# Decode attention with a gated MLP on one core: the first column group of the output moves from partitions 0–3 to partitions 28–31

## The chip, the cores and the metric

The kernel runs on one core of a Trainium2 chip. The metric is device time in microseconds (us) of one execution, the median of several runs. Before the change it is 110.05 us, the median of 3 runs that lie between 110.0 and 110.17 us. One further execution was taken by the hardware profiler; all durations below are from it.

## What is computed

Two batch rows of 448 numbers go through a layer norm, a query projection, attention of 16 query heads over 8 key/value heads with a window of the last 2048 positions, and an output projection. A small MLP on the same normed rows gives a gate, and the output is the input plus attention times gate:

```
xn  = layernorm(x)                                  # x: 2 x 1 x 448
q   = xn @ wq                                       # 16 heads of 256
p   = softmax(q k^T / 16)  over the last 2048 keys  # 8 kv heads, each for 2 query heads
s   = (p v) @ wo                                    # 4096 -> 448
g   = silu( relu(xn @ w1) @ w2 )                    # 448 -> 1792 -> 448
out = x + s * g                                     # bfloat16
```

## The kernel before, in words

The kernel is written as five lists of instructions, one for each engine: TensorE (PE), VectorE (DVE), ScalarE (ACT), GpSimd (POOL) and SyncE (SP). Each instruction names the earlier ones that it depends on, and a small planner (`_Prog`) turns that into semaphores: a transfer has a semaphore of its own that counts to 16, a compute instruction adds one to its engine's semaphore. The order inside a list is the order in which it is written. All matrix products are recorded at one line (311) and all transfer issues at line 39.

**The loads** are all issued by SP in one queue, in this order: wq, w1, w2, four key tiles of 4 MB (two batch rows times two groups of four kv heads), the value tiles into the same buffers as soon as the scores of a tile are done (the last one in two halves), and at the end wo in five parts of 20, 4, 4, 3 and 1 blocks (`WO_PARTS`). ACT issues only the small loads: `x_sb`, the two input rows as they are, and `x_c`, the same rows in the layout of the output.

**The middle** does not change. DVE transposes the keys in place (line 346), PE makes the scores of four tiles, DVE and ACT do the softmax, PE multiplies with the values, and DVE scales the result.

**The layout of the output** is what the change touches. The 448 columns are cut into four groups of 112 (`NCOL`). Group c is written as c = 2k + h. The result lies in PSUM as two blocks of four partitions, one for each h, at partitions 32h to 32h+3; inside a block the partition is 2b + k, where b is the batch row. So partitions 0–3 hold the groups with h = 0, and partitions 32–35 those with h = 1, because a matrix product can write to a column strip of PE that begins at a multiple of 32. The vector work at the end runs over partitions 0 to 35 (`ROWS` = 36).

A row gets into its partition through the stationary operand. `at2` (line 231) holds for each of 32 blocks of wo five columns (`PADW`): 0, b=0, 0, b=1, 0. A slice of four columns that starts at 1 − k puts the two batch rows at places k and 2 + k, with zeros between them (line 540). `fpad` (line 215) is the same for a selection matrix in float32, which folds four partial sums that lie in four strips into one (lines 467 and 535). GpSimd clears both tiles at the start (line 268), as the last of six clears on which other instructions wait as `p_z`.

**The end of the kernel** (lines 520 to 552): the first 24 blocks of wo go through PE as four strips with both batch rows (line 525) into `wbk`; DVE copies that to `wc` (line 528). Then PE adds blocks 24 to 27 in the output's layout (line 540), folds `wc` in (line 535), and adds blocks 28 to 31. Each part of wo is waited for through `landed`. DVE multiplies with the gate (line 546), adds the input (line 548), and the result is stored by two transfers that are issued at the same time, one by SP and one by ACT (line 550), each with four rows of 224 bytes. SP waits for both (line 551), and that is the end of the program.

```
d_o = [pr.dma(eng, half(out, h), out_sb[32 * h:32 * h + 4, :], [v_o]) for h, eng in ((0, SP), (1, ACTE))]
pr.op(SP, None, d_o)
```

Of the kernel before, what the change touches and what calls it, by code (L numbers as in the profile page):

```python
# [5 lines left out]
BF = mybir.dt.bfloat16  # L6
F32 = mybir.dt.float32
# [4 lines left out]
PE, DVE, ACTE, SP, POOL = "pe", "dve", "act", "sp", "pool"  # L12
# [121 lines left out]
def bass_recurrent_scan__sliding_block_cached__dense_activation_relu__decode_kernel(  # L134
# [11 lines left out]
    B, Sq, D = A_x.shape  # L146
# [13 lines left out]
    FC = DFF // 2  # L160
    NCOL = D // 4
    ROWS = 36
    PADW = 5
    WO_PARTS = [20, 4, 4, 3, 1]
    WO_TILED = 24
    WO_FOLD = 28
# [2 lines left out]
    with es:  # L169
        pr = _Prog(nc, es)  # L170

        def named(name, shape, dt):
            return es.enter_context(nc.sbuf_tensor(name, shape, dt))

        def psum(name, shape, dt):
            return es.enter_context(nc.psum_tensor(name, shape, dt))

        def view(t, off, dims, n=128, p0=0):
            width = t.shape[1]
            return bass.AP(t, p0 * width + off, [[width, n]] + dims)  # L180
# [6 lines left out]
        wqo = named("wqo", [128, 32 * D], BF)  # L187
# [10 lines left out]
        f8 = named("f8", [128, 8], F32)  # L198
        asel = named("asel", [128, 72], BF)
        x_sb = named("x_sb", [128, D], BF)  # L200
        x_c = named("x_c", [128, NCOL], BF)
# [10 lines left out]
        h_sb = named("h_sb", [128, 448], BF)  # L212
        zc = named("zc", [128, D], F32)
        wc = named("wc", [128, D], F32)
        fpad = named("fpad", [128, PADW], F32)
        ea = named("ea", [128, NCOL], F32)
        g_sb = named("g_sb", [128, NCOL], F32)
        tmp = named("tmp", [128, NCOL], F32)
        out_sb = named("out_sb", [128, NCOL], BF)
# [8 lines left out]
        rs = named("rs", [128, 2 * NU], F32)  # L228
        pt = [named(f"pt{i}", [128, 512], BF) for i in range(NU)]
        o_odd = named("o_odd", [128, DH], F32)  # L230
        at2 = named("at2", [128, 32 * PADW], BF)

        sbk = [psum(f"sbk{i}", [128, 512], F32) for i in range(2)]
        obk = psum("obk", [128, 512], F32)
# [1 line left out]
        mbk = psum("mbk", [128, 512], F32)  # L236
        qbk = psum("qbk", [128, 512], F32)
        wbk = psum("wbk", [128, 512], F32)
        fbk = psum("fbk", [128, 512], F32)

        def half(t, h):
            return t.rearrange("b s (k h n) -> h (b s k) n", h=2, n=NCOL)[h]

        def kv_src(u, cache):
            b, hg = divmod(u, 2)
# [1 line left out]

        d_x = pr.dma(ACTE, x_sb[0:B, :], A_x[:, 0, :])
        p_xc = pr.op(POOL, lambda e: e.memset(x_c[:, :], 0.0))
        d_xc = [pr.dma(ACTE, x_c[32 * h:32 * h + 4, :], half(A_x, h), [p_xc]) for h in range(2)]  # L250
        wq_src = A_wq.rearrange("r (hf c) -> (r hf) c", hf=2).rearrange("(p s) c -> p (s c)", s=SLOTS)
        w1_src = B_w1.rearrange("r (hf c) -> (r hf) c", hf=2).rearrange("(p s) c -> p (s c)", s=SLOTS)
        w2_src = B_w2.rearrange("(p j) n -> p (j n)", j=14)
# [7 lines left out]
        for u in range(NU):  # L261
# [4 lines left out]
            out=ident[:, :], in_=ident[:, :], compare_op=ALU.not_equal, fill=1.0,  # L266
            base=0, pattern=[[-1, 128]], channel_multiplier=1), [i0])
        p_z = [pr.op(POOL, lambda e, t=t: e.memset(t[:, :], 0.0))
               for t in (fpad, asel, rm, bt, qstat, at2)][-1]
# [4 lines left out]
            out=sd[0:B, 0:1], in0=st2[0:B, 1:2], scalar1=EPS, scalar2=None, op0=ALU.add), [v_ag])  # L274
# [5 lines left out]
        def z(t):  # L280
            return a_z[t.name]

        def red(out, in_, axis=AX.X):
            def fn(e):
                with nc.allow_low_precision("zeros and ones"):
                    return e.tensor_reduce(out=out, in_=in_, axis=axis, op=ALU.add)
            return fn
# [4 lines left out]
        v_pm = pr.op(DVE, red(pmask[:, :], view(ident, 0, [[1, 4], [4, 32]])))  # L292
        v_g8 = pr.op(DVE, red(view(g8, 0, [[2, 4], [1, 2]]), view(ident, 0, [[32, 4], [1, 2], [2, 4]])))
        v_f8 = pr.op(DVE, red(f8[:, :], view(ident, 0, [[1, 8], [8, 16]])))
        v_fp = pr.op(DVE, lambda e: e.tensor_copy(view(fpad, 1, [[2, B]]), f8[:, 0:B]), [v_f8, p_z])
        v_h2 = pr.op(DVE, red(half2[:, :], view(ident, 0, [[8, 2], [16, 8], [1, 8]]), AX.XY))
        v_gs = pr.op(DVE, lambda e: e.tensor_copy(
            view(gsum, 0, [[8, 16], [1, 8]]), view(g8, 0, [[0, 16], [1, 8]])), [v_g8])
# [4 lines left out]
        for e2 in range(2):  # L303
            v_xn = pr.op(DVE, lambda e, e2=e2: e.tensor_scalar(
                out=view(xg, 128 - 127 * e2, [[256, 4], [128, 2], [2, 64]], n=B),
# [4 lines left out]
        def mm(out_ap, lhsT, rhs, start, stop=False, **kw):  # L310
            return lambda e: e.matmul(out_ap, lhsT=lhsT, rhs=rhs, start=start, stop=stop,  # L311
                                      skip_group_check=True, **kw)

        for s in range(SLOTS):
# [3 lines left out]
            out=view(xr, 0, [[4, SLOTS], [2, 2], [1, 2]]), in0=view(mbk, 0, [[2, SLOTS], [0, 2], [1, 2]]),  # L318
# [3 lines left out]
        deps = [d_wq, v_xr, z(qbk)]  # L322
        for s in range(SLOTS):
            for i in range(4):
                lo = s * HC + i * 512
                m_q = pr.op(PE, mm(qbk[32 * i:32 * i + 4, :], xr[:, 4 * s:4 * s + 4], wqo[:, lo:lo + 512],
                                   s == 0, s == SLOTS - 1, tile_position=(0, 32 * i)), deps)
                deps = []
        v_q = pr.op(DVE, lambda e: e.tensor_scalar(  # L329
            out=view(q_x, 0, [[256, 8], [128, 2], [1, 32]]), in0=view(qbk, 0, [[64, 8], [1, 2], [2, 32]]),  # L330
# [3 lines left out]
        deps = [v_qx, st["mbk"]]  # L334
        for n in range(16):
            m_qt = pr.op(PE, mm(mbk[:, 16 * n:16 * n + 16], q_x[:, 128 * n:128 * n + 128],
                                view(ident, 0, [[32, 4], [1, 4]]), n == 0), deps)
            deps = []
# [92 lines left out]
        def do_turn_out(hg):  # L431
            deps = [st["osb", 2 + hg], v_as, st["mbk"]]
            lo = 64 * hg
            for dq in range(8):
                o = pr.op(PE, mm(mbk[lo:lo + 64, 288:352], asel[:, 7 - dq:71 - dq],
                                 view(o_sb, hg * 2 * DH + 32 * dq, [[DH, B], [1, 32]]),
                                 dq == 0, dq == 7, tile_position=(0, lo)), deps)
                deps = []
            st["at"] = st["mbk"] = pr.op(DVE, lambda e: e.tensor_copy(
                view(at2, 1, [[2, B], [PADW, 32]], n=64, p0=lo), view(mbk, 288, [[32, B], [1, 32]], n=64, p0=lo)), [o, p_z])  # L440

        def do_H():
            deps = [st["w1"], v_xr, v_q]
# [12 lines left out]
        def do_F():  # L456
            deps = [st["w2"], st["h"], z(fbk)]
            for j in range(14):
                i = j % 4
                o = pr.op(PE, mm(fbk[32 * i:32 * i + B, 0:D], h_sb[:, 32 * j:32 * j + 2], w2_sb[:, j * D:j * D + D],  # L460
                                 j < 4, j >= 10, tile_position=(0, 32 * i)), deps)
                deps = []
            v = pr.op(DVE, lambda e: e.tensor_copy(zc[:, :], fbk[:, 0:D]), [o])
            deps = [v, v_fp, st["mbk"]]
            for c in range(4):
                k, h = divmod(c, 2)
                o = pr.op(PE, mm(mbk[32 * h:32 * h + 4, 0:NCOL], fpad[:, 1 - k:5 - k],
                                 zc[:, NCOL * c:NCOL * c + NCOL], k == 0, k == 1, tile_position=(0, 32 * h)), deps)
                deps = []
            a_e = pr.op(ACTE, lambda e: e.activation(ea[0:ROWS, :], mbk[0:ROWS, 0:NCOL], ACT.Exp, scale=-1.0), [o])  # L470
            v = pr.op(DVE, lambda e: e.tensor_scalar(
                out=ea[0:ROWS, :], in0=ea[0:ROWS, :], scalar1=1.0, scalar2=None, op0=ALU.add), [a_e])
            v = pr.op(DVE, lambda e: e.reciprocal(tmp[0:ROWS, :], ea[0:ROWS, :]), [v])
            st["g"] = st["mbk"] = pr.op(DVE, lambda e: e.tensor_tensor(
                out=g_sb[0:ROWS, :], in0=mbk[0:ROWS, 0:NCOL], in1=tmp[0:ROWS, :], op=ALU.mult), [v])
# [3 lines left out]

        do_H()  # L480
        do_F()
        pr.mark("dve_tell", eng=DVE)
        do_turn(0, 0, 4)
# [22 lines left out]
        for u in range(NU):  # L506
            do_PV(u)
            if u == 0:
                pr.mark("block2")
            if u in (0, NU - 1):  # L510
                fill(1)
            do_out(u)
            if u >= 2:
                do_turn_out(u - 2)

        landed, j0 = {}, 0
# [5 lines left out]
        deps = [st["at"], z(wbk)]  # L522
        for j in range(WO_TILED):
            i = j % 4
            o = pr.op(PE, mm(wbk[32 * i:32 * i + B, 0:D], view(at2, PADW * j + 1, [[2, B]]), wqo[:, j * D:j * D + D],
                             j < 4, j >= WO_TILED - 4, tile_position=(0, 32 * i)), deps + [landed.get(j)])
            deps = []
        v_wc = pr.op(DVE, lambda e: e.tensor_copy(wc[:, :], wbk[:, 0:D]), [o])  # L528
        pr.mark("late")
        deps = [st["g"]]  # L530
        for j in range(WO_TILED, 32):
            if j == WO_FOLD:
                for c in range(4):
                    k, h = divmod(c, 2)
                    pr.op(PE, mm(fbk[32 * h:32 * h + 4, 0:NCOL], fpad[:, 1 - k:5 - k],
                                 wc[:, NCOL * c:NCOL * c + NCOL], False, tile_position=(0, 32 * h)), [v_wc])
            for c in range(4):
                k, h = divmod(c, 2)
                lo = j * D + c * NCOL
                m_o = pr.op(PE, mm(fbk[32 * h:32 * h + 4, 0:NCOL], at2[:, PADW * j + 1 - k:PADW * j + 5 - k],  # L540
                                   wqo[:, lo:lo + NCOL], j == WO_TILED and k == 0, j == 31,
                                   tile_position=(0, 32 * h)), deps + [landed.get(j)])
                deps = []

        pr.mark("dve_jump", eng=DVE)
# [1 line left out]
            out=tmp[0:ROWS, :], in0=fbk[0:ROWS, 0:NCOL], in1=g_sb[0:ROWS, :], op=ALU.mult), [m_o, st["g"]])  # L547
        v_o = pr.op(DVE, lambda e: e.tensor_tensor(  # L548
            out=out_sb[0:ROWS, :], in0=tmp[0:ROWS, :], in1=x_c[0:ROWS, :], op=ALU.add), [v_t] + d_xc)
        d_o = [pr.dma(eng, half(out, h), out_sb[32 * h:32 * h + 4, :], [v_o]) for h, eng in ((0, SP), (1, ACTE))]  # L550
        pr.op(SP, None, d_o)
        pr.op(PE, None, [v_o])

        pr.run()
# [28 lines left out]
```

## Time and profile before

| What | Value |
|---|---|
| median of 3 runs | 110.05 us (110.0 to 110.17) |
| the profiled execution, its own time | 110.12 us |
| its span, first to last instruction | 108.8 us |
| bytes moved | 44.16 MB, mean 406 GB/s |
| busy share of the span: DVE, PE, ACT, POOL | 57%, 54%, 8%, 2% |
| mean granted clock of PE | 0.843 |

The profiled execution's own time is 1.3 us more than its span: what lies before the first instruction and behind the last. The profile lists, for each group of instructions, how long one took, and what ended the idle time of the engine before it (its releaser). A view in order of time shows the chain of work that ended last, followed back from the end. Another shows all instructions in order of time with the start in us from the span's begin. A line marked "ACTq" or "SPq" is the time in which the engine's sequencer issues a transfer, not the transfer itself. The trace also holds the moments at which the semaphores were counted up, and the start of each packet on the DMA engines.

### The profile page before, as it was taken

Reading aid. Unit: us, or ns where it says so; the run is one execution under the profiler, and the core shown is the slowest. Engines: PE = TensorE matmul, PEld = TensorE weight load, DVE = VectorE, ACT = ScalarE, POOL = GpSimd, SP = SyncE. Lnnn points to the kernel's source line nnn. Section 1 sums busy time; section 2 is a strip of 40 time slices with the busy share of each in tenths; the row PEclk is TensorE's granted clock in tenths of the full one; section 3 lists DMA queues with packets and bytes.
Section 4 is the critical chain, followed back from the end, with each engine's and each line's share of the span. In section 5 each row is a group of like instructions: output and inputs, shape, how many; then the busy total and the mean of one; then the engine's idle time right before and its main releaser. Section 6 shows DMA issues by size and latency. Waiting matters only on the chain.

```text
span 108.8 us, 1117 instructions
## 1 busy us (share of the span) xinstructions
PE 58.9 (54%) x469; PEld 15.7 (14%) x469; DVE 61.5 (57%) x84; ACT 9.0 (8%) x18; POOL 2.1 (2%) x13
## 2 busy tenths in 40 slices
PE   0001295650000069929961995299448967869672
PEld 0000023120000012101200120011033222303131
DVE  2920007644099979999999999940448332204021
ACT  2970000000000000002000200020020000000000
POOL 7000000000000000000000000000000000000000
PEclk9999999995555558995997599679955699999999
DMA  6899999999998999899989998999899899999960
GB/s 165 337 449 390 413 434 486 423 398 494 434 410 386 506 434 410 386 482 458 410 386 482 458 410 386 482 458 410 386 482 458 367 416 428 434 428 448 376 242 1
DMA packets 2487, 44.16 MB, mean 406 GB/s; under 512 B 306, under 2 KB 436, under 8 KB 820
## 3 DMA queue, kind: packets, MB, share of 16 engines
q1 hardware_dynamic: 2456, 44.11, 95.0%
q8 instruction: 3, 0.05, 0.2%
q10 hardware_dynamic: 28, 0.00, 0.0%
HBM read 44.11 MB, written 0.00 MB: 405 GB/s over the span
## 4 chain that ended last, share of the span: by engine, by line
DMA 56%; DVE 28%; PE 8%; SPq 5%; issue 1%
DMA kv<-in_A_k_cache_dram 32%; DVE kv L346 24%; DMA wqo<-in_A_wo_dram 23%; PE sbk L311 7%; SPq L39 5%; PE fbk L311 1%; DVE q_x L375 1%; DVE rm L363 1%; DVE rm_t L365 0%; DVE bias L369 0%; DVE bt L366 0%; DVE tmp L546 0%; DVE out_sb L548 0%
## 5 line engine op out<-in xcount | busy, mean ns | idle before, releaser
L311 PE MATMUL sbk<-kv,qstat 128*8 128x512 bf16 x128 | 30.1, 1086 | 22.8 <-DVE kv L346 22.8
L346 DVE STREAM_TRANSPOSE kv<-kv 128x2048 f32<-128x2048 f32 x16 | 35.6, 2274 | 4.6 <-DMA kv<-in_A_k_cache_dram 4.6
L311 PEld LDWEIGHTS sbk<-kv,qstat 128*8 128x8 bf16 x128 | 5.2, 107 | 46.1 <-DVE kv L346 28.8
L311 PE MATMUL obk<-kv,pt 128*16 128x512 bf16 x128 | 9.5, 441 | 2.6 <-DVE xg L427 1.2
L424 DVE TENSOR_SCALAR o_odd<-obk,rs 128x256 f32<-128x256 f32 x4 | 1.9, 484 | 11.1 <-PE obk L311 11.1
L370 ACT ACTIVATE e_sb<-sbk,bias 128x512 bf16<-128x512 f32 x4 | 2.8, 688 | 51.8 <-DVE bias L369 51.8
L311 PE MATMUL sbk<-kv,f 128*8 128x512 f32 x14 | 7.0, 613 | 0.0
L311 PE MATMUL qbk<-wqo,xr 128*4 128x512 bf16 x28 | 3.2, 626 | 4.2 <-DMA wqo<-in_A_wq_dram 4.2
L363 DVE TENSOR_REDUCE rm<-sbk 128x1 f32<-128x512 f32 x4 | 2.6, 662 | 4.7 <-PE sbk L311 4.7
L311 PE MATMUL mbk<-ident,xg 2*128 2x2 bf16 x7 | 0.3, 161 | 8.4 <-issue 8.4
L329 DVE TENSOR_SCALAR q_x<-qbk 128x512 bf16<-128x512 f32 x1 | 0.7, 691 | 7.2 <-PE qbk L311 7.2
L311 PEld LDWEIGHTS obk<-kv,pt 128*16 128x16 bf16 x128 | 3.2, 97 | 8.7 <-issue 5.0
L375 DVE STREAM_TRANSPOSE q_x<-e_sb 128x512 bf16<-128x512 bf16 x4 | 2.8, 691 | 1.7 <-ACT e_sb L370 1.7
L392 DVE TENSOR_TENSOR pt<-spk,pmask 128x512 bf16<-128x512 f32 x4 | 2.6, 684 | 0.8 <-PE spk L311 0.8
L311 PE MATMUL qbk<-w_sb,xr 128*2 128x448 bf16 x28 | 2.8, 572 | 0.0
L528 DVE COPY wc<-wbk 128x448 f32<-128x448 f32 x1 | 0.6, 624 | 3.8 <-PE wbk L311 3.8
L311 PE MATMUL spk<-q_x,perm 128*32 128x128 bf16 x16 | 0.7, 298 | 3.1 <-DVE q_x L375 3.1
L340 DVE CAST qstat<-mbk 32x256 bf16<-32x256 f32 x4 | 1.7, 420 | 0.7 <-PE mbk L311 0.7
L427 DVE SCALAR_TENSOR_TENSOR xg<-obk,rs,o_odd 128x256 bf16<-128x256 f32 x4 | 1.9, 484 | 0.1
L311 PE MATMUL wbk<-wqo,at 128*2 128x448 bf16 x24 | 1.4, 352 | 1.0 <-DMA wqo<-in_A_wo_dram 1.0
L271 DVE BATCH_NORM_STATS2 st<-x_sb 2x6 f32<-2x448 bf16 x1 | 0.6, 616 | 2.0 <-DMA x_sb<-in_A_x_dram 2.0
L311 PEld LDWEIGHTS sbk<-kv,f 128*8 128x8 f32 x14 | 1.3, 96 | 3.1 <-issue 2.6
(72 smaller groups left out, 33.0 us busy)
## 6 DMA issues: line engine op xcount, KB each, us to landing
kv<-in_A_k_cache_dram SPq DMA_DIRECT2D x4, 4096.0 KB, 39.5
kv<-in_A_v_cache_dram SPq DMA_DIRECT2D x3, 4096.0 KB, 22.1
kv<-in_A_v_cache_dram SPq DMA_DIRECT2D x2, 2048.0 KB, 17.6
wqo<-in_A_wq_dram SPq DMA_DIRECT2D x1, 3584.0 KB, 12.2
w_sb<-in_B_w_dram SPq DMA_DIRECT2D x2, 1568.0 KB, 17.1
wqo<-in_A_wo_dram SPq DMA_DIRECT2D x1, 2240.0 KB, 24.4
wqo<-in_A_wo_dram SPq DMA_DIRECT2D x2, 448.0 KB, 25.2
wqo<-in_A_wo_dram SPq DMA_DIRECT2D x1, 336.0 KB, 25.9
```

Source lines behind the costliest of these rows:

```text
L39: o = _Op(eng, lambda e: e.dma_start(dst, src), [d for d in deps if d is not None], True)
L271: v_bn = pr.op(DVE, lambda e: e.bn_stats(st6[0:B, :], x_sb[0:B, :]), [d_x])
L311: return lambda e: e.matmul(out_ap, lhsT=lhsT, rhs=rhs, start=start, stop=stop, skip_group_check=True, **kw)
L329: v_q = pr.op(DVE, lambda e: e.tensor_scalar(out=view(q_x, 0, [[256, 8], [128, 2], [1, 32]]), in0=view(qbk, 0, [[64, 8], [1, 2], [2, 32]]) ...
L340: st["q"] = st["mbk"] = pr.op(DVE, lambda e, Q=Q: e.tensor_copy(qstat[32 * Q:32 * Q + 32, 256 * Q:256 * Q + 256], mbk[32 * Q:32 * Q + 32, ...
L346: st["turn", u] = pr.op(DVE, lambda e, n=n: e.transpose(kf[:, 2048 * n:2048 * n + 2048], kf[:, 2048 * n:2048 * n + 2048]), [d_k[u]])
L363: v = pr.op(DVE, lambda e: e.tensor_reduce(out=rm[:, 0:1], in_=sbk[u % 2][:, :], axis=AX.X, op=ALU.max), [last_S[u], p_z, st.get(("rmt", u ...
L370: st["exp", u] = pr.op(ACTE, lambda e: e.activation(e_sb[:, :], sbk[u % 2][:, :], ACT.Exp, bias=bias[:, 0:1], accum_out=ssum[:, u:u + 1]), ...
L375: st["et", u] = pr.op(DVE, lambda e: e.transpose(q_x[:, 512 * u:512 * u + 512], e_sb[:, :]), [st["exp", u], m_qt])
L392: st["pt", u] = pr.op(DVE, lambda e: e.tensor_tensor(out=view(pt[u], 0, [[8, 64], [2, 4], [1, 2]]), in0=view(spk, 128 * u, [[2, 64], [0, 4 ...
L424: v = pr.op(DVE, lambda e: e.tensor_scalar(out=o_odd[:, :], in0=obk[:, DH:2 * DH], scalar1=rs[:, 2 * u + 1:2 * u + 2], scalar2=None, op0=A ...
L427: st["osb", u] = pr.op(DVE, lambda e: e.scalar_tensor_tensor(out=o_sb[:, lo:lo + DH], in0=obk[:, 0:DH], scalar=rs[:, 2 * u:2 * u + 1], in1 ...
```

## The change

The first block moves from partitions 0–3 to partitions 28–31, so that both blocks form the eight adjacent partitions 28–35. To reach partition 28 in a strip that begins at 0, the stationary operand of the products with h = 0 becomes 32 columns wide (28 of zeros ahead of the four); those with h = 1 keep four columns. For that, each block of `at2` and `fpad` is 32 columns wide instead of five, and the four columns of interest begin at column 29. The copy into `at2` (line 439) therefore writes at a step of 32 elements instead of 5. The accumulation's first product is now chosen by c < 2, which is the same two products as before. `x_c` is loaded by one transfer with eight rows instead of two with four. The output is stored by one transfer with eight rows, issued by ACT; SP issues none and waits for that one. The DRAM side of both transfers walks over h, then over (b, k), then over 112 columns.

```
-    PADW = 5
+    PADW = 32
+    PAD0 = 29
...
-        fpad = named("fpad", [128, PADW], F32)
+        fpad = named("fpad", [128, 2 * PADW], F32)
...
-        at2 = named("at2", [128, 32 * PADW], BF)
+        at2 = named("at2", [128, 33 * PADW], BF)
...
-        def half(t, h):
-            return t.rearrange("b s (k h n) -> h (b s k) n", h=2, n=NCOL)[h]
+        def rows(t):
+            return t.rearrange("b s (k h n) -> h (b s k) n", h=2, n=NCOL)
+
+        def place(t, c, j=0):
+
+            k, h = divmod(c, 2)
+            lo = PADW * j + PAD0 - k
+            return (32 * h, 4, t[:, lo:lo + 4]) if h else (0, 32, t[:, lo - 28:lo + 4])
...
-        d_xc = [pr.dma(ACTE, x_c[32 * h:32 * h + 4, :], half(A_x, h), [p_xc]) for h in range(2)]
+        d_xc = [pr.dma(ACTE, x_c[28:36, :], rows(A_x), [p_xc])]
...
-                view(at2, 1, [[2, B], [PADW, 32]], n=64, p0=lo), view(mbk, 288, [[32, B], [1, 32]], n=64, p0=lo)), [o, p_z])
+                view(at2, PAD0, [[2, B], [PADW, 32]], n=64, p0=lo), view(mbk, 288, [[32, B], [1, 32]], n=64, p0=lo)), [o, p_z])
...
-                k, h = divmod(c, 2)
+                r, n, cols = place(at2, c, j)
                 lo = j * D + c * NCOL
-                m_o = pr.op(PE, mm(fbk[32 * h:32 * h + 4, 0:NCOL], at2[:, PADW * j + 1 - k:PADW * j + 5 - k],
-                                   wqo[:, lo:lo + NCOL], j == WO_TILED and k == 0, j == 31,
-                                   tile_position=(0, 32 * h)), deps + [landed.get(j)])
+                m_o = pr.op(PE, mm(fbk[r:r + n, 0:NCOL], cols, wqo[:, lo:lo + NCOL], j == WO_TILED and c < 2, j == 31,
+                                   tile_position=(0, r)), deps + [landed.get(j)])
...
-        d_o = [pr.dma(eng, half(out, h), out_sb[32 * h:32 * h + 4, :], [v_o]) for h, eng in ((0, SP), (1, ACTE))]
-        pr.op(SP, None, d_o)
+        d_o = pr.dma(ACTE, rows(out), out_sb[28:36, :], [v_o])
+        pr.op(SP, None, [d_o])
```

The folds at lines 467 and 535 change in the same way as line 540, with `fpad` in place of `at2`.

More of the change, by code (lines that the diff above doesn't have):

```diff
@@ L294, in bass_recurrent_scan__sliding_block_cached__dense_activation_relu__decode_kernel @@
         v_f8 = pr.op(DVE, red(f8[:, :], view(ident, 0, [[1, 8], [8, 16]])))
-        v_fp = pr.op(DVE, lambda e: e.tensor_copy(view(fpad, 1, [[2, B]]), f8[:, 0:B]), [v_f8, p_z])
+        v_fp = pr.op(DVE, lambda e: e.tensor_copy(view(fpad, PAD0, [[2, B]]), f8[:, 0:B]), [v_f8, p_z])
         v_h2 = pr.op(DVE, red(half2[:, :], view(ident, 0, [[8, 2], [16, 8], [1, 8]]), AX.XY))
@@ L465, in do_F @@
             for c in range(4):
-                k, h = divmod(c, 2)
-                o = pr.op(PE, mm(mbk[32 * h:32 * h + 4, 0:NCOL], fpad[:, 1 - k:5 - k],
-                                 zc[:, NCOL * c:NCOL * c + NCOL], k == 0, k == 1, tile_position=(0, 32 * h)), deps)
+                r, n, cols = place(fpad, c)
+                o = pr.op(PE, mm(mbk[r:r + n, 0:NCOL], cols, zc[:, NCOL * c:NCOL * c + NCOL], c < 2, c >= 2,
+                                 tile_position=(0, r)), deps)
                 deps = []
@@ L524, in bass_recurrent_scan__sliding_block_cached__dense_activation_relu__decode_kernel @@
             i = j % 4
-            o = pr.op(PE, mm(wbk[32 * i:32 * i + B, 0:D], view(at2, PADW * j + 1, [[2, B]]), wqo[:, j * D:j * D + D],
+            o = pr.op(PE, mm(wbk[32 * i:32 * i + B, 0:D], view(at2, PADW * j + PAD0, [[2, B]]), wqo[:, j * D:j * D + D],
                              j < 4, j >= WO_TILED - 4, tile_position=(0, 32 * i)), deps + [landed.get(j)])
@@ L533, in bass_recurrent_scan__sliding_block_cached__dense_activation_relu__decode_kernel @@
                 for c in range(4):
-                    k, h = divmod(c, 2)
-                    pr.op(PE, mm(fbk[32 * h:32 * h + 4, 0:NCOL], fpad[:, 1 - k:5 - k],
-                                 wc[:, NCOL * c:NCOL * c + NCOL], False, tile_position=(0, 32 * h)), [v_wc])
+                    r, n, cols = place(fpad, c)
+                    pr.op(PE, mm(fbk[r:r + n, 0:NCOL], cols, wc[:, NCOL * c:NCOL * c + NCOL], False,
+                                 tile_position=(0, r)), [v_wc])
             for c in range(4):
-                k, h = divmod(c, 2)
+                r, n, cols = place(at2, c, j)
                 lo = j * D + c * NCOL
-                m_o = pr.op(PE, mm(fbk[32 * h:32 * h + 4, 0:NCOL], at2[:, PADW * j + 1 - k:PADW * j + 5 - k],
-                                   wqo[:, lo:lo + NCOL], j == WO_TILED and k == 0, j == 31,
-                                   tile_position=(0, 32 * h)), deps + [landed.get(j)])
+                m_o = pr.op(PE, mm(fbk[r:r + n, 0:NCOL], cols, wqo[:, lo:lo + NCOL], j == WO_TILED and c < 2, j == 31,
+                                   tile_position=(0, r)), deps + [landed.get(j)])
                 deps = []
```

## The prediction

> **What bounds the kernel now.** I read the DMA row of the slices first, then the chain in order of time, then the last microseconds in the timeline, then SP's own waits.
>
> ```profile
> DMA  6899999999998999899989998999899899999960
> ```
>
> The 16 DMA engines are busy from the first slice to the last but one. 44.16 MB have to come in, and nothing in the change alters the large loads. So the time is the end of the stream of loads and a tail behind it. The chain shows where the tail begins:
>
> ```profile
> 79.80 25.54 DMA wqo<-in_A_wo_dram
> 105.34 0.04 issue
> 105.38 1.42 PE fbk L311 x40
> 106.80 0.02 issue
> 106.82 0.28 DVE tmp L546
> 107.10 0.02 issue
> 107.12 0.27 DVE out_sb L548
> ```
>
> The span ends at 108.8, so 1.4 us lie behind DVE's last instruction. The timeline of the tail, and SP's waits:
>
> ```profile
> 106.22 0.39 PEld L311 LDWEIGHTS fbk<-wqo,at 128*4 128x4 bf16 x16 [0.16 <-DMA wqo<-in_A_wo_dram]
> 106.22 0.56 PE L311 MATMUL fbk<-wqo,at 128*4 128x112 bf16 x16
> 107.42 0.35 SPq L39 DMA_DIRECT2D out_dram<-out_sb  x1
> 107.42 0.27 ACTq L39 DMA_DIRECT2D out_dram<-out_sb  x1
> ...
> SPq L69 <- DMA out_dram<-out_sb: 1.0, 1, 1.0
> ```
>
> Both stores are issued at once, and SP then waits 1.0 us. The trace's counts of the two semaphores tell which store it waits for. ACT's four counts arrive at 108.510, 108.522, 108.548 and 108.588, SP's at 108.693, 108.700, 108.726 and 108.773; SP's final wait closes at 108.796. Yet the packets of both go out together: ACT's four rows start at 108.173 to 108.245, SP's at 108.197 to 108.263. So SP's store leaves 0.02 us later and is counted 0.185 us later, and it alone sets the end. In order, the four pairs differ by 183, 178, 178 and 185 ns: as if each of SP's counts stood behind one of ACT's on the same DMA engine.
>
> **The change, part by part.**
>
> *The store (line 550).* SP's transfer goes; ACT's has eight rows. Terms against the end of before:
> 1. SP's counts are gone and ACT's set the end: 108.773 − 108.588 = −0.185.
> 2. Eight rows in one transfer. The trace has a two-row load with two counts and four-row loads with four, besides an early one each; one whose two sides differ (two by four in DRAM, eight partitions in SBUF) it doesn't have. On two DMA engines each takes four rows. Packets on one engine follow each other by 11 to 13 ns (108.173, 108.184, 108.197, 108.210), so three more rows cost 0.036; but the last of two engines starts at 108.185 instead of the last of four at 108.245, −0.060. Together −0.02. On eight engines with a row each, the spread of starts (0.072 over four) grows to about 0.17: +0.10. I take two engines, the outermost count that both sides can be divided by as in the two-row load: −0.02; ends −0.02 and +0.10.
> 3. The issue. The DRAM side can't be walked in one stride. On SP, V loads (two strides in DRAM against 128 partitions) issue in 0.534 us and flat wo parts in 0.432; size isn't it, the 28,672-byte rows of wq took 0.406. So up to +0.10. But issue time reaches the packets only in part: SP's issue took 0.073 longer than ACT's and its first packet started 0.024 later. Between 0 and +0.10 I take +0.05.
> 4. SP's last wait now has one semaphore. In before it was already open and closed 23 ns after the last count. A single wait takes 50 to 51 ns (DVE at 106.836, PE at 107.428) and SP's began 16 ns after ACT's last count: 66 instead of 23, +0.04.
>
> The sum is −0.185 − 0.02 + 0.05 + 0.04 = −0.115.
>
> The Trainium skill, "DMA: Bandwidth & Descriptors", section "Queues, rings and completion order", says that a semaphore increment lands only after every earlier write of its DMA engine, whichever queue that came from; the four pairs at 0.18 us agree. Its section on why a DMA counts by 16 says that a transfer uses the largest number of engines up to 16 that divides the outermost count of both sides; for 2 and 8 that is two engines, so by it term 2 would be −0.02.
>
> *The wide stationary operand (lines 535, 540).* Half of PE's 40 last weight loads go from 4 to 32 columns: 16 in bfloat16, 4 in float32. These rows bear on it:
>
> ```profile
> L311 PEld LDWEIGHTS fbk<-wqo,at 128*4 128x4 bf16 x32 | 0.8, 84 | 1.2 <-DMA wqo<-in_A_wo_dram 1.2
> L311 PEld LDWEIGHTS mbk<-xg,asel 128*64 128x64 bf16 x16 | 0.7, 111 | 2.8 <-DVE xg L427 2.8
> L311 PEld LDWEIGHTS mbk<-ssum,gsum 128*128 128x128 f32 x2 | 0.5, 310 | 0.2 <-issue 0.2
> ```
>
> 64 columns take 111 ns and 4 take 84: 0.45 ns a column, so 28 more cost 13 ns. In the tail, pairs of products follow each other every 49 ns (their moving operand is 112 columns), and loads run beside products. The 64-column products of `asel` came every 32 ns with their loads, so a 32-column load fits under 49 ns. What shows is the first load behind a wait: +0.013, for the wait on wo's fourth part, which landed at 106.174. The growth ahead of it is swallowed by the 0.16 us that PE waits there. Cost +0.01; ends 0 and the rival below.
>
> *The clears (line 268).* `at2` grows from 160 to 1056 columns: clearing `qstat` (1024) took 0.952 us, `at2` 0.231, so +0.75, and +0.04 for `fpad`. `p_z` moves from 2.89 to about 3.68. The first that needs it, line 295, starts at 4.03. Were it late, DVE's chain to `xg` ends at 6.13 and PE starts on it at 8.41. Cost nothing.
>
> *The copy to `at2` (line 439).* 0.338 us at a step of 10 bytes, 64 after. The last one ends at 100.84, and PE takes `at2` up at 103.2, when wo's first part has landed. A cost up to 2.3 us is hidden; nothing.
>
> *`x_c` (line 250).* One transfer fewer on ACT (0.26 to 0.31 us of issue), ahead of a table load at 1.95 that nothing late waits for; its consumer is line 548. Its rows may lie on two DMA engines instead of four: some 50 ns on an engine, more or less (a row and its count, 16 + 9 ns, twice). If one of these is the engine that ends the stream, ±0.03. Nothing. The folds at 24 us, and the third semaphore at line 548, lie far off the path or under line 546.
>
> **Sum:** −0.115 + 0.01 = −0.10 us. The profiled execution would go from 110.12 to 110.02, its span from 108.8 to 108.7. The median of the runs is 0.07 below the profiled one, so the forecast is 110.05 − 0.10 = 109.95. About 0.2% (0.22 us) is what a measurement of this kernel can tell from no change; the forecast lies inside it.
>
> **Rivals.**
> - *The two issues hinder each other.* ACT's first packet left 478 ns behind the end of its issue, the two-row load's at the start 379 ns. If ACT alone is that quick (−0.10) and the two strides cost nothing (−0.05), the sum is −0.25: 109.80. For it: both sequencers issued within 5 ns. Against: at the start SP was issuing too.
> - *The gain is spread away.* Eight engines (+0.12 against term 2) with the full issue cost (+0.05): +0.07, about no change, 110.1.
> - *Slower: rows wait for rows.* Where two transfers met on one DMA engine, the second's count came 0.18 us later. If that is the price of each write to DRAM behind another of its engine, and not of the counts alone, four rows on an engine cost 3 × 0.18 = 0.54 instead of 0.036: −0.10 + 0.50 = +0.40, 110.45. It decides only if an engine gets more than one row. Against: SP's rows started 24 ns behind ACT's and weren't held back.
> - *Slower: the weight loads are not hidden.* 8 × 13 ns ahead of the wait, and in float32 (310 − 87) / 124 × 28 = 50 ns, four times: 0.30, less the 0.16 that PE waits; then 8 × 13 ns behind it: +0.24 and with the store +0.13, 110.18. The Trainium skill, "TensorE: Matmul & The Clock Gate", section "LDWEIGHTS (loading the stationary operand)", gives a load as columns divided by 1.2 ns; by that estimate 28 columns are 23 ns, and the sum would be about +0.2, if nothing hid them. The 32 ns between products with 64-column loads speak against that.
> - *The instruction pages fall otherwise.* Two DMA engines end every load about 0.8 us behind the others (wq: 12.87 and 12.96, the rest by 11.98), and two pages of 16 KB were fetched at 1.91 and 5.74. Should one land on the other's engine, or be spared, the stream ends some 0.7 us later or earlier: 110.7 or 109.3. PE's list keeps its length, so this is unlikely.
>
> **The numbers.** Forecast 0.55, with a range of its own from 109.83 to 110.08; issues hinder each other 0.17; spread away 0.10; rows wait 0.08; loads not hidden 0.05; pages 0.05. Faster by over 0.2% (below 109.83): most of the second case, 0.14, the low edge of the first, 0.06, half of the pages, 0.02: 0.22. Slower by over 0.2% (above 110.27): rows wait 0.08, pages 0.02, the upper edge of the unhidden loads 0.03: 0.13. Within: 0.65. The range from 109.75 to 110.27 holds the forecast, the quick issue, the spread gain and most of the unhidden loads.
>
> **What would show it.** Right: one store, its counts complete near 108.64 on this span's scale, SP's wait closing some 0.07 later, products in the tail still paired at 49 ns, PE's tail within 0.02 us of 1.42. Wrong: counts of the store more than 0.4 us behind its last packet (rows wait), pairs at 60 ns or more (loads not hidden), an issue on ACT of over 0.4 us, or an end of wo's stream that has moved by more than 0.1 us, which none of these steps can explain.

## The result, and the profile after

The changed kernel takes 110.69 us, the median of 10 runs (110.44 to 111.2). The kernel before, run on the same chips, takes 110.13 us, the median of 10 (110.0 to 110.36). The ratio is 1.0052, with a 95% interval from 1.0033 to 1.007: slower by 0.36 to 0.77 us, where 0.10 us less was forecast. The profiled execution took 110.44 us with a span of 109.1 us; that of before took 110.12 us with 108.8.

The stream of loads is as it was. This is the DMA row of the slices, and the end of the chain in order of time (start us, us, what), both of the changed kernel:

```profile
DMA  5898999999989998999899989998999899999940
```

```profile
79.88 25.42 DMA wqo<-in_A_wo_dram
105.30 0.04 issue
105.34 1.42 PE fbk L318 x37
106.77 0.02 issue
106.79 0.28 DVE tmp L552
107.07 0.02 issue
107.09 0.27 DVE out_sb L554
```

The part of wo that PE's tail starts on lands at 105.30 instead of 105.34, PE's tail lasts 1.42 us as before, and DVE is done at 107.36 instead of 107.39. Up to here nothing is lost. The timeline shows the one transfer that is left, and SP's list of waits the end of it:

```profile
107.39 0.65 ACTq L39 DMA_DIRECT2D out_dram<-out_sb  x1
```

```profile
SPq L69 <- DMA out_dram<-out_sb: 27.8, 1, 27.8
```

The store's issue takes 0.65 us on ACT where it took 0.27. (SP's wait of 27.8 us is long only because SP has nothing to issue any more, and begins to wait at 81 us.) The trace's packets and semaphore counts give the rest, in us from the start of the issue:

| | issue | first packet | last count | SP's wait closes |
|---|---|---|---|---|
| before, ACT's store | 0.274 | 0.752 | 1.167 | |
| before, SP's store | 0.347 | 0.781 | 1.357 | 1.380 |
| after, ACT's store | 0.647 | 1.299 | 1.700 | 1.734 |

From the start of the issue to the end the changed kernel needs 1.734 − 1.380 = 0.354 us more. The whole of it and more lies ahead of the first packet, 1.299 − 0.752 = 0.547 us; behind the first packet the change gains, as it was meant to.

### The profile page after: what moved, and what is told of

The parts are those of the page before. It is cut to its first block, busy times and chain, and to the rows that moved or that the text cites. A ratio compares the mean times of both kernels' runs of the same rounds, so it can differ in the third digit from the quotient of the medians.

```text
span 109.1 us, 1115 instructions
## 1 busy us (share of the span) xinstructions
PE 58.6 (54%) x469; PEld 15.4 (14%) x469; DVE 61.7 (57%) x84; ACT 9.0 (8%) x18; POOL 2.9 (3%) x13
## 4 chain that ended last, share of the span: by engine, by line
DMA 56%; DVE 28%; PE 8%; SPq 5%; issue 1%
DMA kv<-in_A_k_cache_dram 33%; DVE kv L353 24%; DMA wqo<-in_A_wo_dram 23%; PE sbk L318 7%; SPq L39 5%; PE fbk L318 1%; DVE q_x L382 1%; DVE rm L370 1%; DVE rm_t L372 0%; DVE bias L376 0%; DVE bt L373 0%; DVE tmp L552 0%; DVE out_sb L554 0%
```

## The experiments

**Theory 1**: the loss is the issue of the eight-row store, because DRAM has to be walked with two strides. **Theory 2**, the rival: the wide stationary operands, or the eight-row load of the input, move the stream of loads or the tail. All ratios are against the kernel before, run on the same chip, with 95% intervals. "Flat" is a transfer that walks DRAM in one stride. "From issue to end" runs from the start of the last store's issue (the first of the two, where there are two) to the close of SP's last wait. The diffs are against the changed kernel unless said otherwise.

**1. Store in two transfers.**

```
-        d_o = pr.dma(ACTE, rows(out), out_sb[28:36, :], [v_o])
-        pr.op(SP, None, [d_o])
+        d_o = [pr.dma(eng, rows(out)[h], out_sb[28 + 4 * h:32 + 4 * h, :], [v_o]) for h, eng in ((0, SP), (1, ACTE))]
+        pr.op(SP, None, d_o)
```

> The changed kernel with one edit: the result is stored from partitions 28 to 35 by two transfers of four rows again, one issued by SP and one by ACT. Theory 1 (the eight-row store alone is the loss: its issue and the time to its first packet are longer because its DRAM side needs two strides): the issues go back to about 0.35 and 0.27 us, the first packets leave about 0.75 us behind the start of the issue, and the time is that of the kernel before, ratio 0.999 to 1.001. Theory 2 (the wide stationary operands or the eight-row load of the input shift the stream of loads): the time stays at the changed kernel's, ratio 1.004 to 1.006.

Measured 110.34 us, 1.0016 (1.0003 to 1.0028). The timeline:

```profile
107.37 0.35 SPq L39 DMA_DIRECT2D out_dram<-out_sb  x1
107.37 0.28 ACTq L39 DMA_DIRECT2D out_dram<-out_sb  x1
```

The issues are back at 0.347 and 0.282 us, ACT's first packet at 0.759. From issue to end: 1.378 us, against 1.380 before. The tail is as before, with the wide operands in it; the median lies a little above what theory 1 asks, and its interval does not reach down to 1.

**2. Load in two transfers.**

```
-        d_xc = [pr.dma(ACTE, x_c[28:36, :], rows(A_x), [p_xc])]
+        d_xc = [pr.dma(ACTE, x_c[28 + 4 * h:32 + 4 * h, :], rows(A_x)[h], [p_xc]) for h in range(2)]
```

> The changed kernel with one edit: the input in the output's layout is loaded by two transfers of four rows again, the store stays one of eight rows. Theory 1 (the store alone): the same as the changed kernel, ratio 1.003 to 1.006, and the store's issue stays at 0.65 us. Theory 2 (the load with four rows on each of two DMA engines is part of it, and of the wider spread of its runs): the ratio falls by 0.002 or more, and the runs lie within 0.4 us as they did before the change.

Measured 110.74 us, 1.0058 (1.0042 to 1.0074). Nothing is regained without the eight-row load, and the runs still spread over 0.6 us; this is theory 1. Its timeline:

```profile
107.37 0.70 ACTq L39 DMA_DIRECT2D out_dram<-out_sb  x1
```

The issue is even 0.06 us longer than in the changed kernel. Here it is the first transfer with two strides on ACT; in the changed kernel the load of the input was that, and took 0.74 us.

**3. Both in two transfers**, the two diffs above together: only the layout is left of the change.

> The changed kernel with load and store both as two transfers of four rows: only the layout with the wide stationary operands, the larger clears and the 64-byte step of the copy is left of the change. Theory 1: no difference from the kernel before, ratio 0.999 to 1.001. Theory 2, if the layout costs: 1.002 or more, with a later end of the last wo transfer or of the tail on PE.

Measured 110.06 us, 0.9993 (0.9981 to 1.0006). From wo's last count to the start of the issue it takes 1.006 us, against 0.993 before. So the layout is free within 0.013 us, and theory 2's first half falls.

**4. The store on SP.** `d_o = pr.dma(SP, rows(out), ...)`.

> The changed kernel with its one eight-row store issued by SP in place of ACT. Theory 1a (the price hangs on the issuing sequencer; SP issues two-stride transfers all along, in 0.534 us against 0.432): the issue is about 0.45 us, the first packet leaves 0.2 us earlier than with ACT, ratio 1.001 to 1.003. Theory 1b (the price is that of the transfer's shape on any sequencer): the issue stays above 0.6 us and the ratio is 1.003 to 1.006.

Measured 110.78 us, 1.0048 (1.0034 to 1.0063). The timeline:

```profile
107.71 0.77 SPq L39 DMA_DIRECT2D out_dram<-out_sb  x1
```

The issue takes 0.77 us on SP, and the first packet leaves 1.378 us behind the start of the issue. Theory 1b: the price is not ACT's.

**5. Eight rows, flat.** The output's column groups come out in another order.

```
-        d_o = pr.dma(ACTE, rows(out), out_sb[28:36, :], [v_o])
+        d_o = pr.dma(ACTE, out.rearrange("b s (m n) -> (b s m) n", n=NCOL), out_sb[28:36, :], [v_o])
```

> The changed kernel with its eight-row store walking DRAM in one stride: row after row of 224 bytes. The output's column groups come out in another order, nothing else is changed. Theory 1 (the second stride is the price): the issue on ACT falls from 0.65 to 0.3 us, the first packet leaves about 0.75 us behind the start of the issue, and as SP's second store is gone as well the time is a little below the kernel before, ratio 0.998 to 1.000. Rival (eight rows or partitions in a transfer are the price, whatever the strides): issue above 0.6 us, ratio 1.003 to 1.006. The counts tell how many DMA engines a flat eight-row transfer uses: two or eight.

Measured 110.31 us, 1.0007 (0.9992 to 1.0023). The timeline:

```profile
107.53 0.31 ACTq L39 DMA_DIRECT2D out_dram<-out_sb  x1
```

The same eight partitions, the same bytes, the same engine: 0.31 us of issue, the first packet after 0.784 us, the end after 1.258 instead of 1.734. Eight counts arrive, 0.013 us apart, as from eight DMA engines with a row each. Theory 1 holds, and its rival, the number of rows or partitions, falls; the median is again above what the tail gives, since a tail 0.12 us shorter than before's should stand at 0.999.

**6. Four rows, two strides.** As in 3, but each store takes its rows two by two; they come out in another order.

```
-        d_o = pr.dma(ACTE, rows(out), out_sb[28:36, :], [v_o])
-        pr.op(SP, None, [d_o])
+        d_o = [pr.dma(eng, out.rearrange("b s (k h n) -> h k (b s) n", h=2, n=NCOL)[h], out_sb[28 + 4 * h:32 + 4 * h, :], [v_o]) for h, eng in ((0, SP), (1, ACTE))]
+        pr.op(SP, None, d_o)
```

> The changed kernel with load and store as two transfers of four rows, but the store's rows in an order that needs two strides in DRAM (two by two). The output's rows come out in another order, nothing else is changed. Theory 1 (the second stride is the price): both issues grow by 0.3 us or more against 0.35 and 0.27, ratio 1.003 or more. Rival (only the number of rows or a count of outermost rows that differs between the two sides by four matters): issues as in the kernel before, ratio 0.999 to 1.001.

Measured 110.83 us, 1.0056 (1.0043 to 1.0069). The timeline:

```profile
107.35 0.77 SPq L39 DMA_DIRECT2D out_dram<-out_sb  x1
107.36 0.71 ACTq L39 DMA_DIRECT2D out_dram<-out_sb  x1
```

The issues take 0.35 and 0.28 with one stride in 1 and 3. From issue to end it is 2.022 us instead of 1.380. The form with two strides costs, with four rows as with eight.

One thing changes together with the stride in 5 and 6: each two-stride store has two counts, so it runs on two DMA engines, and the flat ones have four or eight. No run varies one without the other. The one transfer with two counts and a single stride is the load of `x_sb`, ACT's first: its issue takes 0.538 us, and its first packet leaves 0.917 us behind the start of the issue. Against the flat store of before (0.274 and 0.752) that is 0.165 us more to the first packet, where the changed kernel's store has 0.547 more. So if a load of two rows may stand in for a store, two engines alone would account for less than a third of the delay. The issue alone does not separate the two: there the load of `x_sb` has 0.264 us more than the flat store, and the changed kernel's store 0.373; that it is ACT's first transfer may be part of it. Several rows on an engine are not the price either: the flat parts of wo, 128 rows with sixteen counts, issue in 0.432 us on SP, where the two-stride stores take 0.77.

**7. The same store once before**, from the input tile at 10.6 us.

```
+            st["pre"] = pr.dma(ACTE, rows(out), x_c[28:36, :], d_xc)
...
-        d_o = pr.dma(ACTE, rows(out), out_sb[28:36, :], [v_o])
+        d_o = pr.dma(ACTE, rows(out), out_sb[28:36, :], [v_o, st["pre"]])
```

> The changed kernel with a store of the same shape issued once by ACT in the first quarter of the run, from the input tile, so that the last store is not the first of its kind. Theory 1c (part of the price is that this form of issue is met for the first time on ACT): the last issue falls from 0.65 us to 0.5 or less, and the ratio by 0.001 or more below the changed kernel's. Rival (the price is paid at each issue): the last issue stays at 0.65 us and the ratio at 1.003 to 1.006.

Measured 110.77 us, 1.0049 (1.0036 to 1.0063). The timeline, early and late:

```profile
10.58 0.64 ACTq L39 DMA_DIRECT2D out_dram<-x_c  x1
...
107.43 0.61 ACTq L39 DMA_DIRECT2D out_dram<-out_sb  x1
```

The last store's issue is 0.04 us shorter than the early one's, and the load at the start, with two strides as well and the first of them on ACT, took 0.74. So 0.06 to 0.1 us belongs to the first time (2 and 7); the rest of the price is paid at each issue.

**8. One flat store of four rows of 448 bytes** (against the kernel before). DVE adds in two steps and brings the second block to partitions 0–3.

```
-        out_sb = named("out_sb", [128, NCOL], BF)
+        out_sb = named("out_sb", [128, 2 * NCOL], BF)
...
-        v_o = pr.op(DVE, lambda e: e.tensor_tensor(
-            out=out_sb[0:ROWS, :], in0=tmp[0:ROWS, :], in1=x_c[0:ROWS, :], op=ALU.add), [v_t] + d_xc)
-        d_o = [pr.dma(eng, half(out, h), out_sb[32 * h:32 * h + 4, :], [v_o]) for h, eng in ((0, SP), (1, ACTE))]
+        for h in range(2):
+            v_o = pr.op(DVE, lambda e, h=h: e.tensor_tensor(
+                out=out_sb[0:4, NCOL * h:NCOL * h + NCOL], in0=tmp[32 * h:32 * h + 4, :], in1=x_c[32 * h:32 * h + 4, :],
+                op=ALU.add), [v_t] + d_xc)
+        d_o = pr.dma(ACTE, out.rearrange("b s (k m) -> (b s k) m", k=2), out_sb[0:4, :], [v_o])
```

> The kernel before with another way to a single store: DVE adds the input in two instructions, of which the second writes from partitions 32 to 35 to 0 to 3 beside the first block, and ACT stores four rows of 448 bytes that lie one after the other in DRAM. Theory 1 (a transfer that DRAM can walk in one stride issues in 0.27 us, and without SP's store its counts stand behind no others): 0.185 us less at the store, 0.13 to 0.3 us more on DVE, so ratio 0.998 to 1.001. Rival (a single store from ACT costs more whatever its shape): 1.003 or more.

Measured 110.25 us, 1.0004 (0.999 to 1.0017). From issue to end 1.203 us, 0.18 less than before; the second addition costs 0.27. As theory 1 has it, and no gain.

**9. The same with GpSimd for the second addition.** The loop's engine becomes DVE for h = 0 and POOL for h = 1, and ACT waits for both.

> The kernel before with a single flat store of four rows of 448 bytes, where DVE adds the input for the first block and GpSimd at the same time for the second, which it writes from partitions 32 to 35 to 0 to 3. If GpSimd needs no more than 0.35 us for it, the second addition of 0.28 us on DVE is saved against the version with both on DVE, and the ratio is 0.997 to 0.999. If GpSimd is slower than 0.55 us or starts late, 1.000 or more.

Measured 110.48 us, 1.0019 (1.0004 to 1.0033). The timeline:

```profile
107.10 0.26 DVE L548 TENSOR_TENSOR out_sb<-tmp,x_c 4x112 bf16<-4x112 f32 x1
107.15 0.47 POOL L548 TENSOR_TENSOR out_sb<-tmp,x_c 4x112 bf16<-4x112 f32 x1 [104.23 <-DVE tmp L546]
107.71 0.27 ACTq L39 DMA_DIRECT2D out_dram<-out_sb  x1
```

GpSimd needs 0.47 us for what DVE does in 0.26, and the issue starts 0.09 us behind its end. That costs a little more than the second step on DVE did: from wo's last count to the start of the issue it takes 1.310 us, against 1.267 in 8. GpSimd's time lies between the two that the expectation named, and the ratio is that of the slower one.

**10. Flat store, load in two transfers** (the diffs of 5 and 2).

> The changed kernel with the flat eight-row store (column groups of the output in another order, nothing else changed) and the input loaded by two transfers of four rows again. So far the kernels with one eight-row load and a flat store stand at 1.0016 and 1.0007, those with two loads at 0.9993. Theory L (the eight-row load costs about 0.2 us in most runs, unseen in the profiled one): ratio 0.997 to 0.9995, below the kernel with the flat store and one load. Theory N (that difference is chance): 0.999 to 1.001, as there.

Measured 110.12 us, 0.9988 (0.9975 to 1.0001). From issue to end 1.239 us, 0.141 less than before. This is the gain that the forecast was after, on a store without a second stride, and with eight DMA engines instead of two. The interval still just reaches 1.

**11. The eight-row load twice**, store in two transfers.

```
+        x_d = named("x_d", [128, NCOL], BF)
...
-        d_xc = [pr.dma(ACTE, x_c[28:36, :], rows(A_x), [p_xc])]
+        d_xc = [pr.dma(ACTE, t[28:36, :], rows(A_x), [p_xc]) for t in (x_c, x_d)]
```

> The changed kernel with the store as two flat transfers of four rows and the eight-row load done twice, the second into a tile of its own that only the last addition waits for. Theory L: twice the price of the load, ratio 1.003 to 1.005. Theory N: 0.999 to 1.0015.

Measured 110.43 us, 1.001 (0.9985 to 1.0034). The price of the load, if there is one, did not double; but the interval holds all of theory N's range and the low end of theory L's.

**12. The changed kernel again.**

> The changed kernel once more, beside the other three on the same chip, for the size: its profiled execution was 0.32 us behind that of before, its median 0.56. If the store's issue and its way to the first packet are the whole price, the ratio is 1.003 to 1.004; if there is more that the profiled execution didn't show, 1.005 or more.

Measured 111.01 us, 1.0054 (1.0035 to 1.0073). The ratio lies with the second case, the interval reaches into the first. From issue to end it is again 1.734 us. The profiled execution took 110.7 us, 0.26 more than the first one, with an identical tail. Where that lies is told in the last section.

**13 to 16. Where some 0.2 us more may come from.** All with the store in two flat transfers. 13 takes the eight-row load to 16.5 us, 14 walks DRAM in one stride in it (the added column groups come in another order), 15 leaves the load out (zeros are added), and 16 is the kernel before with its two loads at 16.3 us:

```
13: st["xc"] = [pr.dma(ACTE, x_c[28:36, :], rows(A_x), [p_xc, m_q])]
14: d_xc = [pr.dma(ACTE, x_c[28:36, :], A_x.rearrange("b s (m n) -> (b s m) n", n=NCOL), [p_xc])]
15: d_xc = [p_xc]
16: st["xc"] = [pr.dma(ACTE, x_c[32 * h:32 * h + 4, :], half(A_x, h), [p_xc, m_q]) for h in range(2)]
```

> The changed kernel with the store as two flat transfers, and the one eight-row load of the input not at the start but after the query projection, some 17 us into the run. In all profiles so far the end of the span is the landing of wq's last part plus a fixed amount for each kernel, and over all runs the kernels with one eight-row load at the start stand about 0.2 us higher than those with two four-row loads. Theory L (the eight-row load among the first loads sets the last DMA engine back): ratio 0.998 to 1.000 here, against 1.0016 with the load at the start. Theory N (chance): 1.000 to 1.002.

> The changed kernel with the store as two flat transfers, and the input loaded at the start by one eight-row transfer that walks DRAM in one stride, so that the issue is short and eight DMA engines take a row each (the column groups of the added input come in another order, nothing else changed). Theory L, second form (the second stride or the four rows on each of two engines are what costs at the start): ratio 0.998 to 1.000. Theory L, first form (one transfer in place of two, whatever its shape), or theory N: 1.001 to 1.002.

> The changed kernel with the store as two flat transfers and without the load of the input in the output's layout: zeros are added instead of the input. Theory L: without it the start is at least as quick as with two four-row loads, ratio 0.997 to 1.000. Theory N: the same as with one load within chance, 1.000 to 1.002.

> The kernel before with its two four-row loads of the input after the query projection. If small loads among the first large ones cost at all, this is below the kernel before: 0.997 to 0.999. If four-row loads cost nothing there, 0.999 to 1.001.

Measured 0.9992 (0.9972 to 1.0012), 1.0019 (0.9995 to 1.0043), 1.0 (0.9982 to 1.0017) and 1.0014 (0.9996 to 1.0032). Every interval holds 1, so none of the four decides. By the ratios alone 13 speaks for theory L and 14 against its second form, 15 lies where both theories meet, and 16 fits neither case. 14 also shows the second stride in a load: this is ACT's queue at the start, with one stride in the second line, and then the same in 11, with two strides in both loads:

```profile
0.73 0.54 ACTq L39 DMA_DIRECT2D x_sb<-in_A_x_dram  x1
1.32 0.28 ACTq L39 DMA_DIRECT2D x_c<-in_A_x_dram  x1
```

```profile
1.33 0.70 ACTq L39 DMA_DIRECT2D x_c<-in_A_x_dram  x1
2.07 0.61 ACTq L39 DMA_DIRECT2D x_d<-in_A_x_dram  x1
```

0.28 us against 0.70 and 0.61 for the same eight rows.

## Why the prediction was wrong, step by step

*The bound, and where the change can act*: right. From wq's last count to wo's last count it takes 93.45 to 93.51 us in all 18 profiled executions, whatever was changed. In these executions only the tail behind it is the change's; what the medians hold beyond that is taken up under what stays open.

*Terms 1 and 2, SP's counts gone and eight rows on two engines (−0.185 − 0.02)*: right. From the first packet to the last count it was 108.773 − 108.173 = 0.600 and is 0.401: −0.199. The eight-row store has two counts (and the early one) and four rows on each of two engines, 0.010 to 0.013 us apart. By the Trainium skill, "DMA: Bandwidth & Descriptors", section "Why a DMA increments its semaphore by 16 and not by 1", a transfer whose sides begin with 2 and 8 runs on two engines, and one whose sides both begin with 8 on eight: the two counts here and the flat store's eight agree.

*Term 3, the issue (+0.05)*: this is the step that failed. It measured +0.547, eleven times as much: 0.373 in the issue itself, and another 0.174 between its end and the first packet (0.652 instead of 0.478). An issue of over 0.4 us on ACT had been named as a sign of being wrong, and it came at 0.647. Two judgements made the term small. The price of a second stride was read from the V loads on SP, 0.534 against 0.432 us; the two-stride stores take 0.61 to 0.77 where flat ones take 0.27 to 0.35. And the longer issue was taken to reach the packets only in part, since SP's packets of before left 0.024 us behind ACT's after an issue 0.073 longer; the packets are later by more than the issue is. The upper end of +0.10 was no bound at all: the trace had no small transfer with two strides, and the row that stood in for it had 128 rows over 16 engines. What makes the second stride so much dearer here than in the V loads, no run tells. Nor is it shown how much of the price is the stride's and how much comes of the two DMA engines that go with it; the load of `x_sb` puts the engines' part of the whole delay below a third, but not of the issue (experiment 6).

*Term 4, SP's last wait (+0.04)*: +0.011. It closes 0.034 us behind the last count instead of 0.023: the wait itself takes 0.017 us, not the 0.050 that was read from other engines' waits. The terms as measured: 0.547 − 0.199 + 0.011 = 0.359, and 0.354 is the difference from issue to end (before, SP's issue began 0.005 us ahead of ACT's).

*The wide stationary operand (+0.01)*: right. Groups of the changed kernel's tail, with the mean ns behind the busy time:

```profile
L318 PEld LDWEIGHTS fbk<-wqo,at 128*32 128x32 bf16 x16 | 0.8, 97 | 1.2 <-DMA wqo<-in_A_wo_dram 1.1
L318 PEld LDWEIGHTS fbk<-wqo,at 128*4 128x4 bf16 x16 | 0.8, 85 | 0.0
L318 PEld LDWEIGHTS fbk<-wc,fpad 128*32 128x32 f32 x4 | 0.4, 110 | 0.0
L318 PEld LDWEIGHTS fbk<-wc,fpad 128*4 128x4 f32 x4 | 0.3, 87 | 0.0
```

12 ns more in bfloat16 (13 were reckoned) and 23 in float32 (the rival had reckoned 50). The pairs of products still follow each other every 49 ns, and the way from wo's last count to the issue grew by 0.015 us. The loads are hidden, and the rival that priced them is out.

*The clears and the copy (nothing)*: right. GpSimd's groups in the changed kernel:

```profile
L275 POOL MEMSET at<- 128x1056 bf16 x1 | 1.0, 977 | 0.0
L275 POOL MEMSET fpad<- 128x64 f32 x1 | 0.2, 151 | 0.0
```

0.977 us against 0.231, and 0.15 against 0.10; the copy into `at2` takes 0.44 us instead of 0.34. Nothing waits for either.

*The rivals*: ACT alone is not quicker (flat, the first packet comes after 0.784 us, against 0.752 beside SP). The rows of one engine do not wait for each other: 0.401 us from first packet to last count leaves no room for three times 0.18. The gain was not spread over eight engines, since two counts came. The instruction pages fell as before: the two early ones were fetched at 1.90 and 5.77 us, before at 1.91 and 5.74, and wo's last count came 0.04 us earlier (106.383 instead of 106.423). That this rival's later end, 110.7, is what was measured is chance. None of the slower rivals came; what made the kernel slower sat inside term 3, which I had bounded at +0.10 and so never made a rival.

*What stays open*: behind wq's last count the changed kernel's profiled execution takes 0.39 us more than that of before, which is a ratio of 1.0035, just inside the interval. The median moved by 0.56, in the repeat by 0.72 (its ratio of 1.0054 is 0.6). If the tails of the other executions are like the profiled ones, the rest lies ahead of wq's last count. To look for it, take from each measured ratio what the kernel's profiled time behind wq's last count gives. Of the eight kernels with the input loaded at the start in eight-row transfers alone, seven are left with 0.0009 to 0.0020 and one with 0.0004, 0.0014 in the mean. Of the nine others, seven lie within 0.0009 of nothing on either side, and two above it, 0.0018 (experiment 2) and 0.0013 (16). That suggests some 0.15 us for the one load in place of two, whatever its strides (14). But doubling it did not double the excess, taking it out of the kernel where it should have shown (2) brought nothing, and no single interval decides. The profiles do not show it either: wq's last count comes at 12.99 us in the mean of these eight kernels, and at 12.98 in the mean of the ten without such a load at the start. So this part is not shown.

No version beat both kernels: 3 and 8 are level with before, and the flat store of 10, whose interval reaches 1 as well, puts the columns in another order.

## What to carry to other kernels

Count the strides of both sides of a transfer before joining two into one. Where the join adds a second stride (and leaves fewer DMA engines, as here), a small transfer at the end of a chain can lose more in its issue (0.37 us here, and 0.55 to the first packet) than the second queue's counts had cost (0.19). A bound taken from rows of another size and shape is no bound: if no row of the trace has the form, leave the range open on that side. And with a span that is fixed from some point on, compare executions from that point, not whole times.

## What the runs showed that was not expected

In the profiled executions, nearly all of the spread that does not come from the tails is made in the first 13 us. PE's first product on wq starts some 0.05 us behind wq's last count (13.173 us in the changed kernel's repeat), and the product on wo's fourth part follows 93.2 us later. These are both lines of the changed kernel's repeat, then of experiment 3, then of experiment 10:

```profile
13.22 0.59 PE L318 MATMUL qbk<-wqo,xr 128*4 128x512 bf16 x4 [4.30 <-DMA wqo<-in_A_wq_dram]
...
106.44 0.57 PE L318 MATMUL fbk<-wqo,at 128*32 128x112 bf16 x16
```

```profile
12.82 1.02 PE L318 MATMUL qbk<-wqo,xr 128*4 128x512 bf16 x8 [4.17 <-DMA wqo<-in_A_wq_dram]
...
106.05 0.57 PE L318 MATMUL fbk<-wqo,at 128*32 128x112 bf16 x16
```

```profile
13.29 0.59 PE L318 MATMUL qbk<-wqo,xr 128*4 128x512 bf16 x4 [4.49 <-DMA wqo<-in_A_wq_dram]
...
106.51 0.57 PE L318 MATMUL fbk<-wqo,at 128*32 128x112 bf16 x16
```

wq's last count lies between 12.78 and 13.24 us over the 18 profiled executions, and wo's last count between 106.25 and 106.71: the same half microsecond, carried through. The difference between the two is the same to 0.05 us in all of them. Executions without a profile can't be split in this way. So a difference of 0.1 us in a tail shows in one profile each, while medians of twelve runs leave it in doubt.
